# End of the feed-forward stage: other PSUM banks for the last groups, earlier input sums, a last round that opens with half products, and an exponential placed behind a copy

## The chip, the core and the metric

The kernel runs on one core of one Trainium2 chip. A core has a matrix engine (TensorE, PE in the profile), a vector engine (VectorE, DVE), an engine for activation functions (ScalarE, ACT), a general engine (GpSimd, POOL) and a queue that issues transfers (SyncE, SP). They run side by side, each through its own list of instructions in a fixed order, and wait for one another by semaphores. PE writes its results to PSUM, which this kernel uses as eight banks of 128 x 512 numbers of 32 bits; the other data lie in SBUF. The metric is the time of one execution on the device in microseconds (us); less is better.

## The reference

Attention with a threshold, then a feed-forward layer with the ELU function. The tokens of the second step are the outputs of the first, eight heads of 64 side by side.

```python
# q, k, v: (8, 8, 576, 64)
scores = scale * np.matmul(q, k.transpose(0, 1, 3, 2))
thresh = np.max(scores, axis=-1, keepdims=True) - tau
scores = np.where(scores >= thresh, scores, -1000000000.0)
attn = np.exp(scores - np.max(scores, axis=-1, keepdims=True))
attn = attn / (np.sum(attn, axis=-1, keepdims=True) + 1e-09)
x = np.matmul(attn, v)            # brought to (4608, 512)
...
h = x @ w_in                      # (512, 2048)
g = np.where(h > 0.0, h, np.exp(np.minimum(h, 0.0)) - 1.0)
return g @ w_out                  # (2048, 512)
```

## The kernel before

Everything is in 32-bit floats. Attention goes by steps (pair of heads, block of 128 queries), 160 in all. The feed-forward layer goes by groups of 512 tokens: group g takes the first 512 tokens of sequence g (0 to 7), and a last group, B (it is 8), takes the 64 tokens that are left of each sequence. Groups 1 to 6 and most of the attention share the time: in the long loop at the end, each step's attention is issued together with a few quarters of matmuls of the feed-forward layer. What follows that loop is matmuls of the feed-forward layer alone: groups B-1 and B, called a and z here.

From group 1 on both matrix products are made of 2 x 2 blocks by a scheme with seven products in place of eight (Winograd's form of Strassen's scheme); the sums that it needs are formed on DVE, POOL and ACT.

- `first_product(g, u)` is one unit of the first product: seven quarters on PE (`product(0)` to `product(6)`), each two matmuls as the program has them and four as the profile counts them. The three banks that it uses are taken from the front of the list `ends` and put back at its end. After a quarter, posts run on the other engines: ACT copies bank 0 to w1 (L860, "w" in the profile), bank 1 to u2 ("u"), bank 2 to s1 ("s"), and then two results to g (L913, L914). POOL adds u2 (L865, u), s1 (s) and t5 (t). DVE adds the last two parts of the result from the banks (L868). `product(3)` writes bank 0 again and so waits for the copy w1.
- ELU of a unit: ACT takes the first exponential (c = 0, L879) and itself subtracts 1 (L884), then the second exponential (c = 1, L879), for which POOL subtracts 1 (L893, "the minus"). DVE then joins exponential and input (L902), once for each c. Buffers ge and km hold exponentials.
- `sums(g, r, c, v)` form four sums for the second product after every second unit (L939, tiles s0 to s3, or in the last rounds spaces that attention has left: qm, e, vm, w, x). While `attending[0]` is true they all go to POOL; after it, only the third of the four does, and the others go to DVE. They are jobs in the list `extra`; `run_extra` takes jobs from it up to a cost, `need_extra` takes the ones that a matmul needs.
- `second_round(g, r)` is half of the second product: for c = 0 and c = 1 seven products (m = 0 to 6) in two quarters each (k = 0, 1), in the order ORDER, which also says which of three banks. After product 0 ACT copies the bank (`snap`, L1004, "s"); DVE and POOL add up the rest (L1008, L1012, L1017, L1019). Quarter k needs the units v up to 2k+1 of the round's four.
- `sums_x(g, rooms)` forms the input sums of a group by five DVE adds (L737 to L739): three new tiles and two blocks changed in place.
- The order of work is written by a small planner. `clock` counts PE's time in quarters of QT = 0.87; `at(t, f)` puts a post on an agenda, ordered by its planned time; `on_pe` first issues what is due. Each engine gets its instructions in the order in which they are issued. So the planned times, 0.1, 0.7 or 1.3 after a quarter's end, set the order in an engine's list, and the semaphores set the real times.
- PSUM: in the long loop the pool "s" has two tiles of two banks for the scores, "f" three banks for the feed-forward layer, "t" one bank for the other products of attention. After the loop all three pools are closed and one pool of six banks is opened (`ends`).
- After the loop the order is: five units of a, `second_round(a, 0)`, units 5 to 7 of a and unit 0 of z, `second_round(a, 1)`, units 1 to 4 of z, `second_round(z, 0)`, units 5 to 7 of z, `second_round(z, 1)`.

Of the kernel before, what the change touches and what calls it, by code (L numbers as in the profile page):

```python
# [10 lines left out]
FP32 = mybir.dt.float32  # L11
# [8 lines left out]
def kernel(  # L20
# [11 lines left out]
    PSUM = bass.MemoryType.PSUM  # L32
    P = 128
    B, H, S, D = q.shape
# [27 lines left out]
    early, late = ExitStack(), {}  # L62
    wstage = early.enter_context(tc.tile_pool(name="wstage", bufs=2))
    wpool = [wstage]
    banks = ExitStack()
    psum = {"t": banks.enter_context(tc.tile_pool(name="ps_t", bufs=2, space=PSUM))}
# [338 lines left out]
    CT = MAIN // 2  # L405
# [6 lines left out]
    def run_extra(budget):  # L412
        while extra and extra[0][0] <= budget:
            cost, _, f = extra.popleft()
            budget -= cost
            f()
# [40 lines left out]
    def bank():  # L457
        return psum["f"].tile([P, 512], FP32, name="f", tag="f")
# [201 lines left out]
    assert units[0][1][0] == 1 and not pending  # L660
    banks.close()
    apart.append(True)
    for name, bufs in (("s", 2), ("f", 3), ("t", 1)):
        psum[name] = banks.enter_context(tc.tile_pool(name=f"ps_{name}2", bufs=bufs, space=PSUM))
    early.close()
    late["x"] = wpool[0] = ctx.enter_context(tc.tile_pool(name="late", bufs=1))

# [65 lines left out]
    def sums_x(g, rooms):  # L733
        (b11, b12), (b21, b22) = ([xts[g][:, k : k + 2, t : t + CT] for t in (0, CT)] for k in (0, 2))
        xs = in_sums["x", g] = rooms
        tt = nc.vector.tensor_tensor
        return [lambda: tt(xs[0], b11, b22, ALU.add), lambda: tt(xs[1], b11, b12, ALU.add),  # L737
                lambda: tt(b12, b12, b22, ALU.subtract), lambda: tt(xs[2], b21, b22, ALU.add),
                lambda: tt(b21, b21, b11, ALU.subtract)]  # L739
# [6 lines left out]
    with tc.manual_schedule():  # L746
# [48 lines left out]
        agenda, clock, now, serial = [], [0.0], [0.0], [0]  # L795

        def at(t, f):
            serial[0] += 1
            heapq.heappush(agenda, (t, serial[0], f))

        def until(t):
            while agenda and agenda[0][0] <= t:
                do_next()
# [5 lines left out]
        def on_pe(cost, f):  # L809
            until(clock[0])  # L810
            f()
            clock[0] += cost
            return clock[0]

        ends = [bank() for _ in range(3)]
# [9 lines left out]
        def first_product(g, u):  # L825
# [23 lines left out]
            def h(j, c):  # L849
                return gs[g, r, c][:, v, j].rearrange("p i t -> p (i t)")  # L850

            def both(c):
                return gs[g, r, c][:, v].rearrange("p j i t -> p (j i t)")

            def place(x):
                return loc["banks"][x]
# [10 lines left out]
            def add(o, x, name):  # L867
                nc.vector.tensor_tensor(o, place(x), loc[name], ALU.add)  # L868

            def exp(c):  # L870

                if attending[0] and (v < RU - 1 or c) and begun[0] + 0.3 < now[0] < begun[0] + 4.4:
                    at(begun[0] + 4.4, lambda: exp(c))
                    return
                e, last = ges.popleft()
                last()
                loc["e", c] = e
                ges.append((e, lambda: elu(c)))
                nc.scalar.activation(e, both(c), AF.Exp)  # L879
                if c:  # L880
                    loc["e1"] = e
                    at(now[0] + 1.6, minus)
                else:
                    nc.scalar.activation(e, e, AF.Copy, bias=-1.0)  # L884
                if attending[0] and (v < RU - 1 or c):
                    late_elus.append((now[0] + 1.2 * c, lambda: elu(c)))
                else:
                    at(now[0] + 1.4, lambda: elu(c))
# [6 lines left out]
            def elu(c):  # L895
                if ("elu", c) in loc:
                    return
                loc["elu", c] = True
                if c:
                    minus()  # L900

                nc.vector.scalar_tensor_tensor(both(c), loc["e", c], 0.0, both(c), ALU.min, ALU.max)  # L902
                ready.add((g, r, c, v))
                if v % 2:
                    sums(g, r, c, v - 1)
# [8 lines left out]
                [(0.1, lambda: nc.scalar.copy(h(1, 0), place(1))),  # L914
                 (0.55, lambda: pool("t5", lambda: h(1, 0), "u2", ALU.subtract))],
                [(0.6, lambda: add(h(0, 0), 2, "t5")), (1.3, lambda: exp(0))],
                [(0.1, lambda: add(h(1, 1), 0, "s1")), (1.4 if attending[0] else 0.7, lambda: exp(1))],
            )
            return [(lambda k=k: product(k), after_[k]) for k in range(7)]

# [28 lines left out]
        waiting, ready, attending = {}, set(), [True]  # L949
# [105 lines left out]
        queue = deque()  # L1055

        def group(g):
            for r in range(2):
                for u in range(RU * r, RU * r + RU):
                    queue.append((first_product, (g, u)))  # L1060
                queue.append((second_round, (g, r)))

        quarters = deque()

        def ffn_quarters(n):
            while n and (quarters or queue):
                if not quarters:
                    f, a = queue.popleft()
                    quarters.extend(f(*a))
                p, posts = quarters.popleft()  # L1070
                end = on_pe(QT, p)
                for lag, f in posts:
                    at(end + lag, f)
                n -= 1
# [73 lines left out]
        for n in range(MIDDLE, len(steps) + 3):  # L1148
            pr, i = divmod(n, NB)
            if n <= len(steps) + 1:  # L1150
                at(clock[0] + 1.5, lambda n=n: fetch(*steps[n - 2]))
            if 0 < n - MIDDLE < 4:
                x = n - MIDDLE - 1
                at(clock[0] + 5.0, lambda x=x: nc.sync.dma_start(wout_sums[0, x], out_sums[x].rearrange("p u n -> p (u n)")))
            if n == MIDDLE + NB:
                ges.append((raw.tile([P, S // T, T], FP32, name="km").rearrange("p j d -> p (j d)")[:, : 2 * CT], lambda: None))
            if n == len(steps):
                at(clock[0], lambda: turn_squares(*steps[-1]))
            if n < len(steps):
                softmax(*steps[n])  # L1160
            b = pr // NPAIR
            if n < len(steps) and pr % NPAIR == 0 and i == 3 and b > 1:
                xs = [late["x"].tile([P, 2, CT], FP32, name=f"x{x}") for x in range(3)]
                jobs = sums_x(b - 1, xs)
                for x, f in enumerate(jobs):
                    at(clock[0] + 4.2 + 0.5 * x + (4.0 if x > 2 else 0), f)
                group(b - 1)
            before, behind_ = QUARTERS[i]
            ffn_quarters(before)
            values_of(*steps[n - 3])  # L1170
            ffn_quarters(behind_)
        ffn_quarters(len(quarters))
        while queue:
            ffn_quarters(1)
            ffn_quarters(len(quarters))
        until(1e9)
        run_extra(99)

        attending[0] = False
        banks.close()
        psum["f"] = ctx.enter_context(tc.tile_pool(name="ps_f3", bufs=6, space=PSUM))
        ends[:] = [bank() for _ in range(6)]
        wide, narrow = wtp.tile([P, 3 * NT, NCH, T], FP32, name="wTb"), wtp.tile([P, 2 * NT, NCH, T], FP32, name="wTa")
        for c, t in enumerate((wide, narrow)):
            flat = t.rearrange("p g c n -> p (g c n)")[:, : RU * 4 * P]
# [8 lines left out]
            more[(1, *divmod(x, 4))] = t[:, : RU * P].rearrange("p (u t) -> p u t", t=P)  # L1196
        xts[B] = xpool.tile([P, KJ, MAIN], FP32, name="xt")
        nc.sync.dma_start(xts[B], xtail.rearrange("j p n -> p j n"))
        xs = [late["x"].tile([P, 2, CT], FP32, name=f"x{x}") for x in range(3)]
        for f in sums_x(B - 1, xs):  # L1200
            f()
        xs = [qkp.tile([P, S], FP32, name="qT") for _ in range(2)] + [qkp.tile([P, TAIL + S], FP32, name="kT")]
        xs = [x[:, : 2 * CT].rearrange("p (k t) -> p k t", k=2) for x in xs]
        late_sums = sums_x(B, xs)
        a, z = B - 1, B
        order = [*((first_product, (a, u)) for u in range(5)), (second_round, (a, 0)),
                 *((first_product, (a, u)) for u in range(5, 8)), (first_product, (z, 0)), (second_round, (a, 1)),
                 *((first_product, (z, u)) for u in range(1, 5)), (second_round, (z, 0)),
                 *((first_product, (z, u)) for u in range(5, 8)), (second_round, (z, 1))]
# [42 lines left out]
```

## Time and profile before

| what | value |
|---|---|
| median of 6 runs | 1390.77 us (1388.02 to 1392.54) |
| the profiled execution | 1391.68 us |
| span of its profile | 1389.9 us |
| mean granted PE clock | 0.994 |
| PE busy, 1200 to 1220 us | 19.68 of 20.00 us |
| PE busy, 1220 to 1240 us | 20.00 of 20.00 us |
| DVE, ACT, POOL busy, 1200 to 1220 us | 13.94, 10.74, 11.29 us |

In this profile the long loop's last scores start at 1149.56, the first unit of a at 1186.49, and the last round at 1358.58. A timeline line gives the start of a group of equal instructions, the time to the end of the last, the engine, the line, output and inputs, the shape, how many, and in brackets the engine's idle time before it and what ended it. A wait on PE moves the end of the kernel as far as nothing later takes it up.

### The profile page before, as it was taken

Reading aid. Unit: us, or ns where it says so; the run is one execution under the profiler, and the core shown is the slowest. Engines: PE = TensorE matmul, PEld = TensorE weight load, DVE = VectorE, ACT = ScalarE, POOL = GpSimd, SP = SyncE. Lnnn points to the kernel's source line nnn. Section 1 sums busy time; section 2 is a strip of 40 time slices with the busy share of each in tenths; the row PEclk is TensorE's granted clock in tenths of the full one; section 3 lists DMA queues with packets and bytes.
Section 4 is the critical chain, followed back from the end, with each engine's and each line's share of the span. In section 5 each row is a group of like instructions: output and inputs, shape, how many; then the busy total and the mean of one; then the engine's idle time right before and its main releaser. Section 6 shows DMA issues by size and latency. Waiting matters only on the chain.

```text
span 1389.9 us, 21954 instructions
## 1 busy us (share of the span) xinstructions
PE 1339.6 (96%) x6566; PEld 991.1 (71%) x6566; DVE 1067.5 (77%) x2362; ACT 633.1 (46%) x1387; POOL 829.6 (60%) x1331
## 2 busy tenths in 40 slices
PE   7897889999999999999999999999999999999998
PEld 4554645746777777777777777777777777888886
DVE  6778885888879887888788878888888874545533
ACT  4665655225444454545353636363535452422421
POOL 4657774778647574757475747665666646524423
PEclk9999999999999999999999999999999999999999
DMA  5235552589798989798888988898979775311211
GB/s 113 58 75 145 144 145 52 167 246 254 220 253 219 275 220 261 217 254 234 243 232 246 255 225 238 228 256 227 249 207 276 221 240 150 130 60 65 91 57 31
DMA packets 316342, 259.82 MB, mean 187 GB/s; under 512 B 208320, under 2 KB 272320, under 8 KB 316224
## 3 DMA queue, kind: packets, MB, share of 16 engines
q1 hardware_dynamic: 316224, 258.42, 67.0%
q8 instruction: 53, 0.87, 0.3%
q14 instruction: 65, 0.53, 0.1%
HBM read 167.84 MB, written 90.51 MB: 186 GB/s over the span
## 4 chain that ended last, share of the span: by engine, by line
PE 77%; DVE 9%; ACT 5%; issue 3%; POOL 3%; DMA 2%; SPq 1%; DVEq 0%; POOLq 0%; ACTq 0%
PE f L999 28%; PE f L846 21%; PE sc L238 12%; PE pv L388 9%; PE f L475 3%; PE pv L384 2%; PE f L435 2%; ACT e L1088 2%; DVE w L265 1%; PE rt L277 1%; ACT e L253 1%; DMA wTa<-there 1%; DVE mx L1078 1%; POOL wtop L143 1%; DVE w L1097 1%
## 5 line engine op out<-in xcount | busy, mean ns | idle before, releaser
L274 POOL TENSOR_SCALAR w<-w,rs 128x576 f32<-128x576 f32 x288 | 246.9, 863 | 108.6 <-DVE rs L1104 75.0
L1078 DVE TENSOR_REDUCE mx<-sc 128x1 f32<-128x576 f32 x207 | 148.1, 752 | 83.7 <-PE sc L238 83.7
L238 PE MATMUL sc<-kT,qT 64*128 64x288 f32 x1024 | 183.9, 442 | 21.6 <-DVE w L265 11.6
L348 DVE STREAM_TRANSPOSE x<-w 128x512 f32<-128x512 f32 (+1 forms) x350 | 182.7, 568 | 8.3 <-POOL w L274 8.3
L1086 ACT ACTIVATE nb<-mx,nkeep 128x1 f32<-128x1 f32 x207 | 61.4, 297 | 253.2 <-DVE mx L1078 253.2
L1088 ACT ACTIVATE e<-sc,nb,keep 128x576 f32<-128x576 f32 x207 | 172.2, 832 | 6.9
L1097 DVE SCALAR_TENSOR_TENSOR w<-sc,th,e 128x576 f32<-128x576 f32 x207 | 163.2, 811 | 8.7 <-ACT e L1088 0.4
L238 PEld LDWEIGHTS sc<-kT,qT 64*128 64x128 f32 x1024 | 101.4, 191 | 86.7 <-issue 51.8
L846 PE MATMUL f<-xt,sw 128*128 128x256 f32 x512 | 129.0, 389 | 1.0 <-DVE ot L1017 0.5
L846 PE MATMUL f<-xt,w_in_sb 128*128 128x256 f32 x512 | 125.1, 383 | 1.7 <-ACT w L860 1.5
L1082 POOL TENSOR_SCALAR th<-mx,ntau 128x1 f32<-128x1 f32 x207 | 54.9, 266 | 112.1 <-DVE mx L1078 111.8
L846 PEld LDWEIGHTS f<-xt,sw 128*128 128x128 f32 x512 | 93.2, 190 | 29.9 <-issue 13.5
L846 PE MATMUL f<-x,w_in_sb 128*128 128x256 f32 x448 | 109.0, 382 | 5.5 <-ACT g L913 5.5
L253 ACT ACTIVATE e<-sc,nb,keep 128x576 f32<-128x576 f32 x81 | 65.2, 831 | 105.1 <-POOL nb L249 104.3
L846 PEld LDWEIGHTS f<-xt,w_in_sb 128*128 128x128 f32 x512 | 95.7, 190 | 22.1 <-ACT xs L400 4.6
L999 PE MATMUL f<-w_out_sb,s 128*128 128x256 f32 x448 | 109.4, 387 | 0.0
L999 PE MATMUL f<-t,s 128*128 128x256 f32 x448 | 106.8, 381 | 0.6 <-POOL s L939 0.6
L999 PE MATMUL f<-w_out_sb,g 128*128 128x256 f32 x448 | 107.2, 382 | 0.0
L846 PEld LDWEIGHTS f<-x,w_in_sb 128*128 128x128 f32 x448 | 84.1, 190 | 21.3 <-ACT g L913 10.3
L999 PEld LDWEIGHTS f<-w_out_sb,s 128*128 128x128 f32 x448 | 82.3, 190 | 23.0 <-issue 13.2
L999 PEld LDWEIGHTS f<-w_out_sb,g 128*128 128x128 f32 x448 | 84.0, 190 | 15.9 <-ACT ge L879 3.5
L999 PEld LDWEIGHTS f<-t,s 128*128 128x128 f32 x448 | 84.0, 190 | 14.3 <-POOL s L939 3.4
(162 smaller groups left out, 2552.1 us busy)
## 6 DMA issues: line engine op xcount, KB each, us to landing
there<-x SPq DMA_DIRECT2D x500, 144.0 KB, 4.2
wTb<-there SPq DMA_DIRECT2D x75, 576.0 KB, 4.7
wTa<-there SPq DMA_DIRECT2D x50, 576.0 KB, 4.4
sw<-win_sums SPq DMA_DIRECT2D x62, 384.0 KB, 4.5
t<-wout_sums SPq DMA_DIRECT2D x45, 512.0 KB, 5.4
qm<-in_q_dram SPq DMA_DIRECT2D x128, 72.0 KB, 4.0
vm<-in_v_dram SPq DMA_DIRECT2D x64, 128.0 KB, 4.1
wst<-in_moe_w_in_dram SPq DMA_DIRECT2D x16, 512.0 KB, 4.4
```

The source lines that it names most:

```text
L238: nc.tensor.matmul(scs[h][:, a, :HALF], qs[r], kT[r, k0 : k0 + HALF], start=True, stop=True)
L253: nc.scalar.activation(e, st[h][:, :, :HALF], AF.Exp, bias=st["nb"][:, h : h + 1], scale=keep)
L274: nc.gpsimd.tensor_scalar(wv, wv, st["rs"][:, h : h + 1], 1.0, ALU.mult, ALU.mult)
L348: nc.vector.transpose(x[:, :, c0 : c0 + nc_], src.rearrange("p (c g n) -> p g c n", c=nc_, n=T))
L388: nc.tensor.matmul(pv[h * D : (h + 1) * D, g0 * T : g1 * T], vm[:, h, c], wT[:, g0:g1, h * (NC + 1) + c], start=False, stop=(c == NC - 1), ...
L846: nc.tensor.matmul(loc["banks"][place], left[:, j], right[:, j], start=(begins and j == 0), stop=(j == 1), skip_group_check=True)
L999: nc.tensor.matmul(place(m), lhs, rhs, start=(begins and v == 0), stop=(v == RU - 1), skip_group_check=True)
L1078: nc.vector.tensor_reduce(st["mx"][:, h : h + 1], st[h][:, :, :HALF], axis=AX.XY, op=ALU.max)
L1082: nc.gpsimd.tensor_scalar(st["th"][:, h : h + 1], st["mx"][:, h : h + 1], 1.0, ntau, ALU.mult, ALU.add)
L1086: nc.scalar.mul(st["nb"][:, h : h + 1], st["mx"][:, h : h + 1], nkeep)
L1088: nc.scalar.activation(e, st[h][:, :, :HALF], AF.Exp, bias=st["nb"][:, h : h + 1], scale=keep)
L1097: nc.vector.scalar_tensor_tensor(wv, sc[:, :, :HALF], st["th"][:, h : h + 1], e, ALU.is_ge, ALU.mult, accum_out=st["sm"][:, h : h + 1])
```

## The change

There are four parts.

1. Banks: of the loop's PSUM pools, "f" is now opened first and stays open. After the loop only "s" and "t" are closed, and their five banks are opened as a new pool; `ends` is those five, followed by the three of "f": eight banks, where there were six.
2. Input sums of group a: the five adds are put on the agenda before the last quarters of the round ahead of it, with planned times from 2.0 us on, 1.5 apart. `attending[0]` becomes false at the same place, and one quarter at a time is issued, with `run_extra(0.9)` after each.
3. The last round (`second_round` of B, 1) issues its first seven quarters in another order: the first halves of products 0, 1 and 3, then the second halves of 0 and 1, then both halves of product 2.
4. The second exponential of units outside the attention loop is planned 1.1 after the unit's last quarter, not 0.7. The next unit's copy w1 is planned 0.97 after it.

```diff
-    for name, bufs in (("s", 2), ("f", 3), ("t", 1)):
-        psum[name] = banks.enter_context(tc.tile_pool(name=f"ps_{name}2", bufs=bufs, space=PSUM))
+    for name, bufs, stack in (("f", 3, ctx), ("s", 2, banks), ("t", 1, banks)):
+        psum[name] = stack.enter_context(tc.tile_pool(name=f"ps_{name}2", bufs=bufs, space=PSUM))
...
-                [(0.1, lambda: add(h(1, 1), 0, "s1")), (1.4 if attending[0] else 0.7, lambda: exp(1))],
+                [(0.1, lambda: add(h(1, 1), 0, "s1")), (1.4 if attending[0] else 1.1, lambda: exp(1))],
...
                     f, a = queue.popleft()
-                    quarters.extend(f(*a))
+                    mine = f(*a)
+
+                    if (f, a) == (second_round, (B, 1)):
+                        mine = [mine[x] for x in (0, 2, 6, 1, 3, 4, 5)] + mine[7:]
+                    quarters.extend(mine)
...
-        ffn_quarters(len(quarters))
-        while queue:
+        attending[0] = False
+        xs = [late["x"].tile([P, 2, CT], FP32, name=f"x{x}") for x in range(3)]
+        for x, f in enumerate(sums_x(B - 1, xs)):
+            at(clock[0] + 2.0 + 1.5 * x, f)
+        while quarters or queue:
             ffn_quarters(1)
-            ffn_quarters(len(quarters))
+            run_extra(0.9)
         until(1e9)
         run_extra(99)
...
-        attending[0] = False
         banks.close()
-        psum["f"] = ctx.enter_context(tc.tile_pool(name="ps_f3", bufs=6, space=PSUM))
-        ends[:] = [bank() for _ in range(6)]
+        psum["f"] = ctx.enter_context(tc.tile_pool(name="ps_f3", bufs=5, space=PSUM))
+        ends[:] = [bank() for _ in range(5)] + ends
...
-        xs = [late["x"].tile([P, 2, CT], FP32, name=f"x{x}") for x in range(3)]
-        for f in sums_x(B - 1, xs):
-            f()
```

## The prediction

> **What bounds the kernel now.** I read the page's busy shares first, then the waits of TensorE (PE) over the last 240 us, where the edits lie, then the timelines of PE, ScalarE (ACT), VectorE (DVE) and GpSimd (POOL) there.
>
> ```profile
> PE 1339.6 (96%) x6566; PEld 991.1 (71%) x6566; DVE 1067.5 (77%) x2362; ACT 633.1 (46%) x1387; POOL 829.6 (60%) x1331
> ```
>
> PE is the bound: only its idle time can be won. In the part that changes it is idle in a few places:
>
> ```profile
> 1180.52 1.99 PE L999 MATMUL f<-t,s 128*128 128x256 f32 x8 [0.28 <-POOL s L939]
> 1186.49 1.99 PE L846 MATMUL f<-xt,sw 128*128 128x256 f32 x8 [0.52 <-DVE ot L1017]
> 1207.79 1.99 PE L846 MATMUL f<-xt,w_in_sb 128*128 128x256 f32 x8 [0.32 <-ACT w L860]
> 1256.76 1.99 PE L846 MATMUL f<-xt,w_in_sb 128*128 128x256 f32 x8 [0.35 <-ACT w L860]
> 1306.09 1.99 PE L846 MATMUL f<-xt,w_in_sb 128*128 128x256 f32 x8 [0.32 <-ACT w L860]
> 1355.03 1.99 PE L846 MATMUL f<-xt,w_in_sb 128*128 128x256 f32 x8 [0.32 <-ACT w L860]
> 1361.41 0.70 PE L999 MATMUL f<-w_out_sb,wTb 128*128 128x256 f32 x2 [1.37 <-DVE wTb L902]
> ```
>
> The reader is to see one wait on POOL, one where the banks are laid out anew, four on the copy w, one in the last round. Each costs more than its idle time: eight undisturbed matmuls start every 1.73 us (1189.18 to 1190.91), and after a wait the first eight take 0.10 longer (1.99 against 1.89). From start to start the slips are 0.54 (1180.52), 0.78 (1186.49), 0.59 at three of the w waits, 0.62 at 1256.76 with a further 0.39 at 1263.20 that only shows as a late start, and 1.64 at 1361.41 (the second product starts at 1361.95 instead of 1360.31, counted from 1358.58). Sum 5.74 us: the most that the edits can win.
>
> Why is w late? A unit of first_product is seven products of 0.865 us, 6.05 us on PE. Beside it runs a loop over three engines:
>
> ```profile
> 1205.67 0.63 ACT L879 ACTIVATE ge<-g 128x512 f32<-128x512 f32 x1 [2.10 <-DVE g L868]
> 1206.33 0.63 ACT L884 ACTIVATE ge<-ge 128x512 f32<-128x512 f32 x1
> 1206.87 0.61 ACT L879 ACTIVATE km<-g 128x512 f32<-128x512 f32 x1
> 1207.39 0.35 ACT L860 COPY w<-f 128x256 f32<-128x256 f32 x1
> 1207.64 0.37 ACT L860 COPY u<-f 128x256 f32<-128x256 f32 x1
> 1211.55 0.63 ACT L879 ACTIVATE ge<-g 128x512 f32<-128x512 f32 x1 [1.36 <-DVE g L868]
> 1218.34 0.63 ACT L879 ACTIVATE km<-wTb 128x512 f32<-128x512 f32 x1 [2.10 <-DVE wTb L868]
> 1220.05 0.35 ACT L1004 COPY s<-f 128x256 f32<-128x256 f32 x1
> ```
>
> From one first exponential to the next it takes 5.88 us (1205.67 to 1211.55), and 6.79 (to 1218.34) in a unit that also forms the sums of second_round. Two units take 12.67 where PE needs 12.10: the loop, not the place of w alone, makes w late. On POOL and DVE:
>
> ```profile
> 1213.45 0.62 POOL L893 TENSOR_SCALAR ge<-ge 128x512 f32<-128x512 f32 x1 [2.45 <-ACT ge L879]
> 1214.03 0.73 POOL L865 TENSOR_TENSOR u<-u,w 128x256 f32<-128x256 f32 x1
> 1214.84 1.06 POOL L865 TENSOR_TENSOR s<-s,u 128x256 f32<-128x256 f32 x1
> 1214.10 1.21 DVE L902 SCALAR_TENSOR_TENSOR g<-ge,g 128x512 f32<-128x512 f32 x1 [0.53 <-POOL ge L893]
> 1215.23 0.94 DVE L939 TENSOR_TENSOR s<-g 128x256 f32<-128x256 f32 x1
> 1217.83 0.41 DVE L868 TENSOR_TENSOR wTb<-f,t 128x256 f32<-128x256 f32 x1
> ```
>
> The reader is to see that the minus (L893) runs while ACT makes the copies w and u, so that it costs the loop nothing, and that POOL and DVE take turns when both work in SBUF: L902 takes 1.21 here and 0.69 at 1212.88 with POOL idle. Read from the ends, a POOL add in turn with DVE adds 0.59, a DVE sum 0.28, L902 0.55.
>
> **The edits, one by one.**
>
> Banks and input sums: the first product after the loop gets a bank that the scores left at 1155.4 (the last mask) instead of one freed by the last ot add. Gain 0.78 at the most; I take all. The five L737 to L739 adds (0.69 each) move among the last adds of the round before, where DVE has idle stretches of 1.30, 1.92 and 1.23 before single adds (1180.28, 1182.62, 1184.28): price 0 under that cover; without it up to 0.69 for one that lands ahead of an add for which a bank waits. They issue no DMA; SP's order is unchanged. The switch before the loop gets other banks too: there PE waits only 0.92 (265.86, on a mask): between -0.9 and +0.9, taken as 0 because it is the steady wait on masks and not on banks.
>
> Jobs taken after each quarter: the two POOL sums at 1179.74 now stand ahead of the add t of 1179.06, and two other sums go to DVE: the wait at 1180.52 goes, 0.54.
>
> Exponential behind the copy: the second exponential moves from ahead of w to behind it. Its followers move too: the program now has POOL do the u add first, then the minus. Counted from the start X of a first exponential by the rows above: L884 at 0.66, w at 1.20 (was 1.72), second exponential at 1.46, u copy at 1.98, ended 2.35 (it waited for the exponential before as well), u add 2.44 (0.09 as from 1213.36 to 1213.45), minus 3.14 (0.70, half of the pair of 1.41 at 1179.74), ended 3.76. The minus has left its cover and stands in the loop: s begins at 3.72, and L902 meets s and t instead of u and s. In a plain unit: s ends 0.69 after the minus, L902 +0.55, t +0.59, then 0.03 to the DVE add and 0.52 to the exponential: X + 6.14 (was 5.88). With sums: s 0.69, L902 0.55, POOL sum 0.59, DVE sum 0.28, t 0.59, DVE sum 0.28, third DVE sum 0.29, 0.51 to the exponential: X + 7.54 (was 6.79). In a round with r=1 the unit behind a sum unit has one more POOL sum ahead of s (row 1257.80, 1.18): 0.69+0.55+0.59+0.28+0.59+0.55 gives 7.0 (was 6.45). This could be less: if DVE and POOL did not meet, s, sum and t take 0.69+0.70+0.70 and the sum unit 6.39. So 6.4 is one end; the other is a full L902 of 0.69 in place of each 0.55, 7.7. I take 7.54, since the rows show the turns in every unit.
>
> Carried through, P being a unit's first matmul (w is needed at P+2.59, and frees PE at X+1.60): group a,0. Unit 1: X=P+6.34. Unit 2: 6.34+7.54-6.05=P+7.83; w of unit 3 late by 7.83+1.60-6.05-2.59=0.79, with restart 0.89. Unit 3: next P+0.98, w in time. Unit 4: the round's start m plus 0.98+7.54-6.05=2.47. There ACT copies s (L1004) only behind both exponentials, 1.71 later (1218.34 to 1220.05), and PE may go on at m+2.47+2.11=m+4.58; its third product is due at m+3.46. Before, that copy ended 0.45 early (1220.40 against 1220.85); now it is 1.12 late, 1.22 with restart. Sum 2.11 against 0.59: +1.52, and the same in z,0. Group a,1: w late by 0.79 and 0.95, snap by 1.13, 2.87 against 1.01: +1.86.
>
> Halves of three products: before, the matmul that needs the last L902 stands 1.30 after the round's start, now 3.03. The first exponential of the last unit starts at m+1.84 by the same count and its L902 ends 2.07 later (1359.34 to 1361.41), m+3.91: 0.98 late with restart instead of 1.64. But product 4 reuses bank 0 with one half-product (0.865) between, not two, and DVE now has the second L902 ahead of the sums: the add that frees the bank comes 0.3 late, 0.4 with restart (0 to 0.9, by the four queued adds of 0.41). With w (0.79): 2.17 against 2.23, -0.06.
>
> Sum: -0.78 -0.54 +1.52 +1.52 +1.86 -0.06 = +3.5 us. Profiled span 1389.9 becomes 1393.4; its execution took 1391.68, 0.9 over the median of 1390.77. I add the difference to the median: 1394.3.
>
> [...]
>
> **Rivals.** A: POOL and DVE meet less in the new order, because L902 now follows later and s runs ahead of it. Place: POOL's s, sum and t. Sum unit 6.39: unit 2 at P+6.6, w early by 0.4, every wait goes: 1390.77-5.74=1385.0. It decides where the sum unit stays below about 7.0: each 0.1 us of it is worth some 0.7 us of span (0.2 in each of three groups, 0.1 in the last), so 3.5 us are gone at 7.04. For it: w does come 0.52 sooner. Against: 0.94, 1.06 and 1.21 in the row of every sum unit. B: half of that, sum unit about 7.0: 1390.8, no change. C: the same turns, but longer: L902 holds POOL for its whole 0.69, the sum unit takes 7.7 (0.16 more, 1.1 us) and the plain unit, lengthened by as much, no longer catches up (as much again), and the late bank of the last round costs its 0.9: 1394.3+1.1+1.1+0.5=1397.
>
> **How the numbers follow.** A measurement of this kernel can't tell 0.2% (2.8 us) from no change. Forecast 0.60 (its own range 1392.5 to 1396; 0.47 of it is over 2.8 us), C 0.12, B 0.14 (all within), A 0.14 (0.13 faster). So slower 0.59, same 0.28, faster 0.13. The range 1388.3 to 1397 leaves out most of A and the top of C.
>
> **What would show it.** Right: no wait at the first product after the loop; POOL's L893 behind L865 u; first exponentials about 7.5 us apart in sum units; w waits of 0.6 to 0.8 still there; a new wait of about 1 us on ACT s L1004 in the third product of three rounds. Wrong: sum units at 6.8 or less, or no waits on s.

## The result, and the profile after

| | before | after |
|---|---|---|
| median of the runs | 1389.70 us (67 runs, 1386.27 to 1393.80) | 1392.97 us (30 runs, 1389.40 to 1395.20) |
| ratio after to before | | 1.0023, 95% interval 1.0017 to 1.0029 |
| profiled execution, its span | 1391.68, 1389.9 us | 1393.00, 1391.2 us |
| from the start of the last group of L388 to the end of the span | 215.68 us | 219.53 us |

The changed kernel is slower by 0.23%: 3.27 us between the medians, where 3.5 were forecast. Whether this is more than the 0.2% that the prediction named as the limit is not settled by the interval; that it is slower is settled.

The last row is the measure that the rest of this text uses. L388 is the last product of attention, so what lies behind it is only the stage that the edits touch. Its place moves between single executions (1168.84 to 1175.31 us in the twelve profiles of this study, with no order by version), and whole spans inherit that. The earliest and the latest are the executions with the highest and the lowest mean granted clock of the span (e7 0.997, e6 0.987; the others 0.990 to 0.994); what moves the others is open. The stretch behind it doesn't move so: in three pairs of kernels whose code is the same up to the last round (before and e10, after and e5, e1 and e9 below), its stages up to there agree within 0.02 us. The profile gives the span to 0.1 us, so the last stage and the stretch as a whole are good to about 0.1.

The page's first row of after; PE's busy time is what it was (1339.6 before), so the loss is idle time:

```profile
PE 1339.4 (96%) x6566; PEld 990.4 (71%) x6566; DVE 1064.3 (77%) x2364; ACT 632.1 (45%) x1387; POOL 825.2 (59%) x1329
```

PE's timeline of after, from the end of the loop on: the first unit of group a, and every group of matmuls with a wait.

```profile
1182.72 1.89 PE L846 MATMUL f<-xt,sw 128*128 128x256 f32 x8
...
1204.27 1.99 PE L846 MATMUL f<-xt,w_in_sb 128*128 128x256 f32 x8 [0.67 <-ACT w L860]
1218.48 1.99 PE L999 MATMUL f<-w_out_sb,g 128*128 128x256 f32 x8 [0.93 <-ACT s L1004]
1254.76 1.99 PE L846 MATMUL f<-xt,w_in_sb 128*128 128x256 f32 x8 [0.62 <-ACT w L860]
1261.73 1.99 PE L846 MATMUL f<-xt,w_in_sb 128*128 128x256 f32 x8 [0.66 <-ACT w L860]
1269.83 1.99 PE L999 MATMUL f<-w_out_sb,wTb 128*128 128x256 f32 x8 [0.93 <-ACT s L1004]
1306.08 1.99 PE L846 MATMUL f<-xt,w_in_sb 128*128 128x256 f32 x8 [0.58 <-ACT w L860]
1320.28 1.99 PE L999 MATMUL f<-w_out_sb,g 128*128 128x256 f32 x8 [0.93 <-ACT s L1004]
1356.55 1.99 PE L846 MATMUL f<-xt,w_in_sb 128*128 128x256 f32 x8 [0.60 <-ACT w L860]
1363.98 0.70 PE L999 MATMUL f<-w_out_sb,wTb 128*128 128x256 f32 x2 [0.69 <-DVE wTb L902]
1368.38 1.99 PE L999 MATMUL f<-w_out_sb,qm 128*128 128x256 f32 x8 [0.24 <-DVE ot L1019]
```

The reader is to see four things. The waits on POOL's s and at the first unit are gone. The waits on w have about doubled (0.32 to some 0.63). Three rounds have a wait on ACT's copy s that they didn't have. In the last round 1.37 has become 0.69 and 0.24.

ACT in one unit with sums, from its first exponential at 1208.77 to the next at 1216.36:

```profile
1208.77 0.63 ACT L879 ACTIVATE ge<-g 128x512 f32<-128x512 f32 x1 [2.10 <-DVE g L868]
...
1209.96 0.35 ACT L860 COPY w<-f 128x256 f32<-128x256 f32 x1
1210.22 0.63 ACT L879 ACTIVATE ge<-g 128x512 f32<-128x512 f32 x1
1210.75 0.36 ACT L860 COPY u<-f 128x256 f32<-128x256 f32 x1
...
1216.36 0.63 ACT L879 ACTIVATE km<-wTb 128x512 f32<-128x512 f32 x1 [3.58 <-DVE wTb L868]
...
1218.07 0.35 ACT L1004 COPY s<-f 128x256 f32<-128x256 f32 x1
```

w does come sooner, counted from the first exponential (1.19 in place of 1.72), and the copy s still comes 1.71 behind one. But the exponentials are 7.59 us apart, where they were 6.79. POOL and, in the second fence, DVE in the same unit:

```profile
1211.19 0.72 POOL L865 TENSOR_TENSOR u<-u,w 128x256 f32<-128x256 f32 x1 [2.97 <-ACT u L860]
1211.88 0.62 POOL L893 TENSOR_SCALAR ge<-ge 128x512 f32<-128x512 f32 x1
1212.46 0.72 POOL L865 TENSOR_TENSOR s<-s,u 128x256 f32<-128x256 f32 x1
1213.14 1.17 POOL L939 TENSOR_TENSOR s<-g 128x256 f32<-128x256 f32 x1
1214.28 0.91 POOL L865 TENSOR_TENSOR t<-wTb,u 128x256 f32<-128x256 f32 x1
```

```profile
1212.53 1.21 DVE L902 SCALAR_TENSOR_TENSOR g<-ge,g 128x512 f32<-128x512 f32 x1 [1.74 <-POOL ge L893]
1213.66 0.94 DVE L939 TENSOR_TENSOR s<-g 128x256 f32<-128x256 f32 x1
1214.63 0.83 DVE L939 TENSOR_TENSOR s<-s,g 128x256 f32<-128x256 f32 x1
1215.50 0.42 DVE L939 TENSOR_TENSOR s<-g,s 128x256 f32<-128x256 f32 x1
1215.85 0.42 DVE L868 TENSOR_TENSOR wTb<-f,t 128x256 f32<-128x256 f32 x1
```

The minus (L893) now stands behind the add u, and DVE waits for it 1.74 us. Before, POOL did it while ACT made its copies. From there on the chain runs without a gap through both engines to L868, for which the next exponential waits.

Here is where the time went, stage by stage, worked out from PE's timelines: each column runs from the first matmul of a stage to that of the next.

| | last L388 to first unit | a: 5 units | round a,0 | 4 units | round a,1 | z: 4 units | round z,0 | 3 units | last round to end | sum |
|---|---|---|---|---|---|---|---|---|---|---|
| before | 12.27 | 30.90 | 24.18 | 25.19 | 24.17 | 24.76 | 24.18 | 18.71 | 31.32 | 215.68 |
| after | 11.05 | 31.21 | 25.37 | 25.98 | 25.37 | 25.09 | 25.37 | 19.00 | 31.09 | 219.53 |
| difference | -1.22 | +0.31 | +1.19 | +0.79 | +1.20 | +0.33 | +1.19 | +0.29 | -0.23 | +3.85 |
| forecast | -1.32 | +0.30 | +1.22 | +0.73 | +1.13 | +0.30 | +1.22 | +0.20 | -0.26 | +3.52 |

Of the forecast 0.78 at the first unit, 0.10 is the longer first group behind the wait, which falls in the second column here. Divided as the measured times are, the forecast is -1.22 and +0.20 for the first two columns: the gain at the first unit was exact, and the five units were 0.11 longer than forecast.

### The profile page after: what moved, and what is told of

It is laid out like the page before. It is cut to its first block, busy times and chain, and to the rows that moved or that the text cites. A ratio compares the mean times of both kernels' runs of the same rounds, so it can differ in the third digit from the quotient of the medians.

```text
span 1391.2 us, 21973 instructions
## 1 busy us (share of the span) xinstructions
PE 1339.4 (96%) x6566; PEld 990.4 (71%) x6566; DVE 1064.3 (77%) x2364; ACT 632.1 (45%) x1387; POOL 825.2 (59%) x1329
## 4 chain that ended last, share of the span: by engine, by line
PE 73%; DVE 10%; ACT 6%; POOL 4%; issue 3%; DMA 2%; SPq 1%; DVEq 0%; POOLq 0%; ACTq 0%
PE f L999 28%; PE f L846 18%; PE sc L238 11%; PE pv L388 8%; PE pv L384 2%; PE f L435 2%; PE f L475 2%; DVE w L265 2%; ACT e L1092 2%; ACT e L253 1%; DVE mx L1082 1%; PE rt L277 1%; DMA there<-x 1%; POOL wtop L143 1%; DVE mx L248 1%
## 5 line engine op out<-in xcount | busy, mean ns | idle before, releaser
L865 POOL TENSOR_TENSOR u<-u,w 128x256 f32<-128x256 f32 x64 | 48.6, 759 | 106.3 <-ACT u L860 106.3
```

## The experiments

"The stretch" is the time from the start of the last L388 group to the end of the span. The ratio is to runs of the kernel before on the same chip, with its 95% interval; one thousandth is 1.39 us. An interval is 2.6 to 5.8 us wide, so that effects of about 1 us are read from the stretch, which is one execution but is free of the loop's scatter.

| kernel | median, us (runs) | ratio to before | stretch, us | stretch against before |
|---|---|---|---|---|
| e1_no_exp | 1386.14 (9) | 0.9979 (0.9969 to 0.9990) | 213.05 | -2.63 |
| e2_exp_only | 1397.25 (6) | 1.0053 (1.0040 to 1.0066) | 222.18 | +6.50 |
| e3_minus_first | 1387.70 (11) | 0.9988 (0.9979 to 0.9998) | 214.72 | -0.96 |
| e4_minus_late | 1381.35 (11) | 0.9951 (0.9937 to 0.9965) | 209.88 | -5.80 |
| e5_no_halves | 1395.01 (12) | 1.0025 (1.0012 to 1.0039) | 222.45 | +6.77 |
| e6_join_late | 1384.41 (6) | 0.9945 (0.9924 to 0.9966) | 210.99 | -4.69 |
| e7_before_late | 1387.50 (12) | 0.9972 (0.9958 to 0.9985) | 212.46 | -3.22 |
| e8_banks_only | 1388.96 (12) | 0.9981 (0.9967 to 0.9995) | 216.42 | +0.74 |
| e9_banks_sums | 1386.63 (12) | 0.9980 (0.9970 to 0.9990) | 214.16 | -1.52 |
| e10_halves_only | 1389.20 (12) | 0.9996 (0.9984 to 1.0008) | 214.41 | -1.27 |

### e1: all but the exponential's new place

```diff
-  (1.4 if attending[0] else 1.1, lambda: exp(1))
+  (1.4 if attending[0] else 0.7, lambda: exp(1))
```

> The change without its fourth part: the second exponential stands ahead of the copy w1 again (0.7 in place of 1.1). Theory (the minus and its turns with L902 have been put into the loop by the fourth part): first exponentials 6.8 us apart in units with sums, as before; no wait at the first product after the loop (-0.78), none on POOL near 1180 (-0.54), the last round's 1.64 gone but 0.4 for a late bank; the waits on w stay. Sum -2.6 us against the kernel before, so about -5.9 against the changed one. Rival 'other parts' (the eight banks, the jobs after each quarter or the half products cost the time): still 3 us slower than before. Rival 'copies' (the loss is that u is copied later on ScalarE): as the theory, -2.6.

Measured: the stretch is 2.63 shorter than before. The first exponentials are 6.79 apart again, as ACT of e1 shows (the third line is the copy w of the unit behind):

```profile
1194.58 0.63 ACT L879 ACTIVATE km<-g 128x512 f32<-128x512 f32 x1 [1.36 <-DVE g L868]
...
1201.37 0.63 ACT L879 ACTIVATE ge<-g 128x512 f32<-128x512 f32 x1 [2.10 <-DVE g L868]
...
1203.09 0.35 ACT L860 COPY w<-f 128x256 f32<-128x256 f32 x1
```

On PE, w is waited for by 0.30 to 0.32 four times, and no round waits for s. So parts 1 to 3 win, and what makes the changed kernel slow is in part 4.

### e2: the exponential alone, in the kernel before

```diff
-  (1.4 if attending[0] else 0.7, lambda: exp(1))
+  (1.4 if attending[0] else 1.1, lambda: exp(1))
```

> The kernel before with the fourth part alone (1.1 in place of 0.7). Theory: units with sums 7.5 us, plain ones 6.1; waits on w of 0.6 to 0.8, new waits of about 1 us on the copy s of three rounds, and in the last round 2.7 in place of 1.64, as nothing covers it: 1.52+1.52+1.86+0.2+1.07 = +6.2 us, 5 to 6.5. Rival 'other parts': not slower than before, faster by the w waits (2.4 us).

Measured: +6.50. Sum units take 7.58 to 7.68; w is waited for by 0.59 to 0.68 five times, s by 0.93 or 0.94 three times, and the last round waits 2.42 for L902. The first of the waits on s:

```profile
1218.24 1.99 PE L999 MATMUL f<-w_out_sb,g 128*128 128x256 f32 x8 [0.93 <-ACT s L1004]
```

This and e1 agree: from e1 to the changed kernel it is 219.53 - 213.05 = +6.48.

### e3: the changed kernel with the minus back under its cover

The minus is planned ahead of the add u; the exponential stays behind the copy w.

```diff
-  at(now[0] + 1.6, minus)
+  at(now[0] + (1.6 if attending[0] else 0.9), minus)
```

> The changed kernel, with the minus issued ahead of the next unit's add u on GpSimd, as before; ScalarE keeps the new order, with the exponential between the copies w and u. Theory: minus 2.16 to 2.78 after the first exponential, u from 2.75 (2.48 before), so units with sums 7.06 us, plain ones under 6.05; small waits of 0.2 to 0.5: about -2 us against before, -5 against the changed kernel. Rival 'copies': the loop stays at 7.5 and the time 3 us over before, as ScalarE's order has not changed.

Measured: 4.81 less than the changed kernel, -0.96 against before. POOL in a sum unit of e3, whose first exponential is at 1208.71:

```profile
1210.88 0.62 POOL L893 TENSOR_SCALAR ge<-ge 128x512 f32<-128x512 f32 x1 [2.72 <-ACT ge L879]
1211.46 0.73 POOL L865 TENSOR_TENSOR u<-u,w 128x256 f32<-128x256 f32 x1
1212.26 1.05 POOL L865 TENSOR_TENSOR s<-s,u 128x256 f32<-128x256 f32 x1
```

The minus waits for the exponential and not for u, and the sum unit takes 7.05 (1208.71 to 1215.76). So of the 0.80 by which part 4 lengthened the sum unit, 0.54 is the minus that left its cover. The other 0.26 is, within 0.01, the copy w itself: the second exponential, and so all that follows it, now stands behind it (it starts 1.45 after the first one, where it started 1.20 after it). The rival 'copies', by which the loop would have stayed at 7.5, falls with it: ACT's order is that of the changed kernel here. The gain is smaller than was expected (-0.96 for -2), and two places show it. The three rounds take 24.64, 24.83 and 24.65, still 1.60 longer together than in e1 (24.17, 24.18, 24.17), with waits on the copy s; and the last round takes 0.76 more than in e1, with waits of 0.43 on L902 and 0.24 on the late bank.

### e4: minus and second join behind the add t

On POOL the minus comes behind u, s and t, so that nothing of the loop waits for it; on DVE the second L902 comes behind L868.

```diff
-  at(now[0] + 1.6, minus)
+  at(now[0] + (1.6 if attending[0] else 4.1), minus)
...
-  at(now[0] + 1.4, lambda: elu(c))
+  at(now[0] + (5.3 if c and not attending[0] else 1.4), lambda: elu(c))
```

> The changed kernel, with the minus and the join L902 of the second exponential moved behind t5 and behind the two DVE adds of the next unit (4.1 and 5.3 after the exponential, in place of 1.6 and 1.4). Theory: GpSimd has u, s, sum, t without the minus and without L902 between; units with sums 6.3 to 6.4 us, plain ones bound by TensorE; no wait on w, none on s, none in the last round: all of the 5.74 us are won, -5 to -6 against before. Rival 'copies': at least 2 us slower than before. If the late join makes a sum or a matmul late, a wait on DVE L902 or L939 shows in the rounds and the gain is smaller.

Measured: -5.80, the fastest of all by the stretch and by the median, and faster than both kernels of this case. POOL in a sum unit of e4:

```profile
1209.77 0.73 POOL L865 TENSOR_TENSOR u<-u,w 128x256 f32<-128x256 f32 x1 [2.40 <-ACT u L860]
1210.57 0.79 POOL L865 TENSOR_TENSOR s<-s,u 128x256 f32<-128x256 f32 x1
1211.33 0.91 POOL L939 TENSOR_TENSOR s<-g 128x256 f32<-128x256 f32 x1
1212.19 0.72 POOL L865 TENSOR_TENSOR t<-wTb,u 128x256 f32<-128x256 f32 x1
1212.88 0.61 POOL L893 TENSOR_SCALAR ge<-ge 128x512 f32<-128x512 f32 x1
```

The reader is to see that the minus has gone to the end, and that s follows u at once. The sum unit takes 6.12 (1207.34 to 1213.46) and the plain unit ahead of it 5.96 (1201.38 to 1207.34); the two together, 12.08, are just under the 12.10 that PE needs. PE shows no wait from the first unit of a on: five units take 30.22, four 24.17, three 18.13, which is what the matmuls take.

### e5: the changed kernel without the halves

The two lines that reorder the last round's quarters are taken out (part 3).

> The change without its third part: the last round begins with whole products again. Theory: the loop as in the changed kernel (7.5 and 6.1 us); the last L902 then ends about 2.6 behind the matmul that needs it, 2.7 with restart, in place of 0.8 with the halves and 0.5 for the late bank: +1.3 us against the changed kernel, +4.7 against before. If the halves win nothing or the late bank takes it all back, it is as slow as the changed kernel.

Measured: 2.92 more than the changed kernel, more than expected. All stages up to the last round agree with after within 0.01 us; the last takes 34.02 in place of 31.09. PE in it, of e5:

```profile
1363.96 0.96 PE L999 MATMUL f<-w_out_sb,wTb 128*128 128x256 f32 x2 [2.42 <-DVE wTb L902]
1364.71 3.36 PE L999 MATMUL f<-t,wTb 128*128 128x256 f32 x8
```

and of e2, which has the same wait:

```profile
1363.82 0.70 PE L999 MATMUL f<-w_out_sb,wTb 128*128 128x256 f32 x2 [2.42 <-DVE wTb L902]
1364.36 1.89 PE L999 MATMUL f<-t,wTb 128*128 128x256 f32 x8
```

Eight matmuls that wait for nothing take 3.36 in the one and 1.89 in the other. The view by windows of e5 (length; busy time of PE, PEld, DVE, ACT, POOL; then PE's granted clock, DMA share, GB/s) says why; the last line is that of e2 for one of the windows:

```profile
1362.00:1364.00 2.00, 0.04 (x1) 0.04 (x1) 0.88 (x3) 1.67 (x3) 0.21 (x1) 1.00 0.00 0
1364.00:1366.00 2.00, 2.00 (x6) 1.61 (x7) 1.97 (x3) 0.37 (x1) 1.26 (x2) 0.56 0.00 0
1366.00:1368.00 2.00, 2.00 (x7) 1.62 (x6) 0.48 (x2) 0.00 (x0) 0.00 (x0) 0.58 0.00 0
...
1364.00:1366.00 2.00, 2.00 (x10) 1.77 (x11) 1.97 (x4) 0.37 (x1) 1.12 (x2) 1.00 0.00 0
```

After the idle stretch the mean granted clock was 0.56 and 0.58 in two windows (1.00 again from 1368 on); in e2 it was 1.00 in the same windows. The last round takes 34.02 here and 32.35 in e2, 1.67 us less. As e2 has the same wait at full clock, I put these 1.67 down to this execution and not to the version, from one execution of each. Without it the halves are worth 2.92 - 1.67 = 1.25 in the presence of part 4, and e5 is 5.10 over before (4.7 expected). The runs don't show these 1.25 by themselves: e5's ratio, 1.0025, is that of the changed kernel, 1.0023, and its interval allows 1.25 more as well as none.

### e6: the changed kernel with the second join alone moved

The exponential stays behind w and the minus between u and s, where the change put it; only the second L902 goes behind L868 (the second hunk of e4).

> The changed kernel, with the join L902 of the second exponential alone moved behind the next unit's two DVE adds (5.3 after the exponential, in place of 1.4); the minus stays between u and s. It tells apart the two halves of the 0.75 us that a unit with sums lost: the minus in the loop and the turns of L902 with GpSimd's s and t. If both count (theory): s 0.69, DVE sum 0.28, sum 0.59, DVE sum 0.28, t 0.59, DVE sum 0.29 behind the minus, units with sums 6.9 to 7.0, plain ones 5.7, about -3.4 us against before. If the minus alone counts: units with sums 7.4 or more, still slower than before. If the turns alone count: units with sums 6.8 or less and -5.5 us, as with both moved.

Measured: -4.69 against before, and 8.54 less than the changed kernel. DVE of e6 around the end of a sum unit:

```profile
1217.14 0.42 DVE L868 TENSOR_TENSOR wTb<-f,t 128x256 f32<-128x256 f32 x1 [1.98 <-POOL t L865]
1217.48 0.41 DVE L868 TENSOR_TENSOR wTa<-f,s 128x256 f32<-128x256 f32 x1
1217.81 0.68 DVE L902 SCALAR_TENSOR_TENSOR g<-ge,g 128x512 f32<-128x512 f32 x1
```

POOL in that unit:

```profile
1214.85 0.89 POOL L865 TENSOR_TENSOR s<-s,u 128x256 f32<-128x256 f32 x1
1215.70 0.72 POOL L939 TENSOR_TENSOR s<-g 128x256 f32<-128x256 f32 x1
1216.39 0.72 POOL L865 TENSOR_TENSOR t<-wTb,u 128x256 f32<-128x256 f32 x1
```

and ACT:

```profile
1210.97 0.63 ACT L879 ACTIVATE ge<-g 128x512 f32<-128x512 f32 x1 [1.60 <-DVE g L868]
...
1212.17 0.35 ACT L860 COPY w<-f 128x256 f32<-128x256 f32 x1
```

L902 takes 0.68 and no longer meets POOL; POOL's sum takes 0.72 in place of 1.17 and its t 0.72 in place of 0.91. The sum unit is down from 7.59 to 6.68 (1210.97 to 1217.65). So L902's turns with POOL cost the sum unit 0.91 and the minus a further 0.56 (6.68 against 6.12 in e4). Neither expectation fits in both numbers: by the unit it is "the turns alone" (6.8 or less), by the time it lies between the two, and e4 shows that the minus counts too. Both are real, but in time they don't add up evenly: with the first, 8.54 us go, and with the second, from e6 to e4, another 1.11 (about 0.7 in the four units behind round a,0 and round a,1, 0.4 in the last round). e6 (6.68) and e1 (6.79) have nearly the same sum unit, but w ends 1.55 after the first exponential in e6 and 2.07 after it in e1, and PE waits for w in e1 and shows no such wait in e6. That is what part 4 is for; how much of it is the copy's earlier place isn't shown, because e6's plain unit is also shorter (5.66 against 5.88).

### e7: the kernel before with minus and second join moved

The two hunks of e4 in the kernel before, with 4.5 and 5.7 for 4.1 and 5.3.

> The kernel before, with the minus and the join of the second exponential moved behind t5 and the DVE adds (4.5 and 5.7 after the exponential), and nothing of the change. Theory: units with sums 6.3 us instead of 6.8, no wait on w; the wait at the first product after the loop (0.78), the one on GpSimd near 1180 (0.54) and 1.3 of the last round's 1.64 stay: -3 us against before. Rival (the w waits come from the place of the exponential on ScalarE, which is as before here): waits on w of 0.3 stay and the time is as before.

Measured: -3.22. The sum units take 6.10 to 6.13, one 6.31, and no wait on w is left; those on POOL's s, on the first unit's bank and on L902 in the last round (0.28, 0.52, 0.83) stay. Adding the -2.63 of parts 1 to 3 gives -5.85, and e4 has -5.80. So with the followers out of the loop it seems to make no difference whether the exponential stands ahead of w or behind it; this is a sum of two runs, and no kernel with parts 1 to 3 and these two hunks alone was run.

### e8, e9, e10: the other parts by themselves

e8 has part 1 alone; e9 parts 1 and 2; e10 part 3. Their edits are those hunks of the diff shown above.

> The kernel before with the first part alone (eight banks, five of them new). The input sums stay behind the round's last adds on DVE, and their fifth add ended at 1189.69, when product 4 would be due at 1189.27 without the wait of 0.78: the wait moves there, 0.4 to 0.9 with restart. Expected: no change, -0.4 to +0.3 us, with a wait on DVE xt L739 at the first unit's fifth product. If the banks alone win the 0.78: -0.8 us and no wait there.

> Parts 1 and 2 alone (banks, input sums, jobs after each quarter; exponential and last round as in the kernel before). Theory, the two first terms of the prediction: the waits at 1180.52 (POOL s, 0.54) and at the first product after the loop (0.78) are gone and nothing takes their place; the four w waits of 0.32 and the wait on L902 in the last round (1.37) stay. 1.3 us less than before; from the start of the last L388 group to the end 214.4 us, where the kernel before has 215.7. Rival: the five DVE adds or the rearranged sums delay a bank or a copy in the round ahead, so that a new wait stands there: between 0 and 1.3 us less, 214.4 to 215.7.

> Part 3 alone (first halves of three products at the start of the last round, all else as in the kernel before). Theory, the prediction's last term: the slip of 1.64 on L902 in the last round becomes 0.4 or less, on the bank that a DVE add frees late (0.16 to 0.3 shown idle): 1.2 us less than before or a little more; from the start of the last L388 group to the end 214.3 to 214.5 us against 215.7. Rival: the late bank costs its upper bound of 0.9, or the wait on L902 only moves to a later half: 0 to 0.7 us less, 215.0 to 215.7.

Of e8, the first wait of PE in group a:

```profile
1185.76 1.10 PE L846 MATMUL f<-xt,w_in_sb 128*128 128x256 f32 x4 [1.19 <-DVE xt L739]
```

The bank is there, but the input sums are not: the wait moves on to the unit's fifth product and grows from 0.52 to 1.19. The expectation counted on the 0.69 for each add that the kernel before has here (1188.28, 1189.00). In group z of the kernel before, the last two of the five adds run beside POOL's first two adds of the unit (1243.99 and 1244.93) and take 1.22 and 1.10 (1244.04 and 1245.29); I put the length of e8's wait down to such a meeting. The stretch is 0.74 longer than before, outside of what was expected (-0.4 to +0.3). The runs of e8 and the kernel before, on the other hand, differ by -0.7 to -4.6 us; the stretch of one execution and this interval don't agree, and which of them is nearer to the truth for e8 stays open.

It bears on a term that the prediction took as 0, between -0.9 and +0.9: part 1 also changes the banks at the switch ahead of the long loop, which the stretch doesn't see. The wait that it named there is the same in both profiles, 0.92 on a mask (at 265.86 before, at 264.18 after). But by the ratios all eight kernels with part 1 come out 0.3 to 3.4 us better than their stretch says; of the three without it two come out worse and one better. A small gain of part 1 ahead of the stretch is possible, and isn't shown.

e9: -1.52 (-1.3 expected). From the last value product to the first unit it is 11.04, as in after; so parts 1 and 2 gain together, and neither of the waits is left. PE of e9 keeps four waits on w of 0.30 or 0.31, and in the last round:

```profile
1355.00 0.70 PE L999 MATMUL f<-w_out_sb,wTb 128*128 128x256 f32 x2 [1.37 <-DVE wTb L902]
```

e10: -1.27 (-1.2 expected). In its last round one short wait is left, on the bank that a DVE add frees:

```profile
1364.48 1.99 PE L999 MATMUL f<-w_out_sb,qm 128*128 128x256 f32 x8 [0.17 <-DVE ot L1019]
```

The terms add up: -1.52 (e9) and -1.27 (e10) make -2.79, where e1, which has all three parts, has -2.63; with the +6.50 of e2 they make +3.71, where the changed kernel has +3.85.

## Why the prediction was right

- **Banks, input sums and jobs after each quarter, -0.78 and -0.54.** Measured -1.22 in the stretch up to the first unit. With the 0.10 that falls behind the first unit that is the -1.32. The adds hide as assumed. But the two edits are one: e8 shows that the bank alone only exposes the next wait.
- **The loop, 7.54, 6.14 and 7.0.** Measured 7.58 to 7.60, 6.11 and 6.97. The step that carried this was to follow the program's order past the moved instruction: the exponential went 0.4 later in planned time, the minus went with it, and so came to stand behind u. e3 shows the minus alone at 0.54. What a sum unit is worth in time was put too low, which the forecast didn't use but rival A did: some 0.7 us for each 0.1, where e3 has 4.81 for 0.54 and e6 8.54 for 0.91, about 0.9 (their plain units are shorter too). Rival A (POOL and DVE meet less, 6.39) falls with the row of the sum unit: L902 1.21, POOL's sum 1.17, DVE's 0.94. Rival C (7.7 and a plain unit as much longer) falls with the same row, B (7.0) too.
- **The copy s, 1.12 late and 0.10 of restart in three rounds.** Measured 1.09 and 0.10 at 1218.48 (due 1217.39); the rounds are 1.19, 1.20 and 1.19 longer. This wait did not exist before, and e1 and e2 tie it to part 4: it is nowhere in e1 and in all three rounds of e2.
- **The last round, -0.06 with its w.** Measured +0.29 - 0.23 = +0.06. L902 is waited for by 0.69, the late bank by 0.24. The halves are worth 1.27 alone (e10) and 1.25 beside part 4 (e5, less the clock; the last round is good to about 0.1).
- **Sum, +3.5.** Measured +3.85 in the stretch and +3.27 between the medians. The forecast of 1394.3 lies 1.3 above the measured 1392.97; 1.07 of that is the median of six runs (1390.77) to which the sum was added, where 67 runs give 1389.70. That the medians come within 0.3 of the sum is in part luck: the stretch has 0.33 more than forecast, and about 0.6 the other way lies ahead of it, where nothing was forecast and no run shows a cause.

What a turn of POOL and DVE adds the prediction read from the rows of before: 0.55 for L902, 0.59 for a POOL add, 0.28 for a DVE sum. The runs keep to these. In the two fences of after above, the ends of the instructions alternate between the two engines: s on POOL ends at 1213.18, L902 at 1213.74, POOL's sum at 1214.31, DVE's at 1214.60, t at 1215.19, DVE's next at 1215.46. Each adds less than its time in after with the other engine idle: L902 0.56 and not 0.69 (1210.09), a POOL add 0.57 to 0.59 and not 0.72 (1211.19), a DVE sum 0.27 to 0.29 and not 0.42 (1215.50). With the whole time for each turn the unit would, by my estimate from these differences, have been longer than the 7.59 measured.

The most that these edits can win was right too: 5.74 us by the prediction, and e4 wins 5.80. It does so with the parts of the change as they are, only that the minus, which the change drew into the loop, and the second join are planned behind the loop.

## What to carry to other kernels

Where a planner orders work by planned times, moving one instruction moves all that is planned relative to it: write down the new order of every engine, and look for a follower that has left its cover for a loop. In a loop over several engines whose period is near that of the bound engine, take out what the loop doesn't wait for (here a subtraction and a join) before moving what it does wait for. And of a wait that is removed, ask what is due next: a free bank was worth nothing until the inputs were there too.

## What the runs showed of the hardware

- The clock after a wait. In e5 a wait of 2.42 us on PE, which had been busy up to it (3.54 of the 4 us from 1358 to 1362), was followed by a mean granted clock of 0.56 (1364 to 1366) and 0.58 (1366 to 1368), and its last round took 1.67 us longer than that of e2, where the same wait, with PE busy up to it as well (3.40 of these 4 us), left the clock at 1.00. A low clock is seen earlier too, behind shorter waits: from 66 to 75 us it was 0.50 in the kernel before and 0.52 in after, where no wait of PE from 50 us on had been over 0.75 us. What decides it isn't shown.
- Two engines in turn. In the two fences of after, where DVE and POOL both work in SBUF, an instruction adds some 0.14 us less to the other engine's than it takes alone (0.69 and 0.56, 0.72 and 0.58, 0.42 and 0.28), for the three kinds that meet here. So for these three the cost of a meeting came out as the other instruction's time less that amount.
